# A four-layer attention and MLP kernel: three row tiles of layer 3 turned by DMA, its last residual rows in spent weights, and tile 5's key sums of layer 1 moved between tile 7's transposes and tile 6's second key half

## The chip, the cores and the metric

The kernel runs on one core of one Trainium2 chip. The metric is the time of one execution in microseconds of device time (us), as the median of several runs. Beside the runs there is one profiled execution, whose trace the views below are taken from.

## What is computed

The input x has 2048 rows of 576 numbers in bf16. Four layers are applied in the order A, B, A, B, each with its own layer norm in front and a residual sum behind. Both A layers share one set of weights, and so do both B layers.

```python
def A(x, wqkv, wo):                       # x: [2048, 576], 32 heads of 18
    q, k, v = split(x @ wqkv)
    phi = lambda t: where(t > 0, t + 1, exp(t)) + 1e-6
    pq, pk = phi(q), phi(k)
    kv = einsum("hsd,hse->hde", pk, v);  z = pk.sum(rows)
    return (pq @ kv) / (pq . z + 1e-6) @ wo      # by head
def B(x, w1, b1, w2, b2):                 # F = 4608
    return gelu(layernorm(x) @ w1 + b1) @ w2 + b2
x = x + A(layernorm(x)); x = x + B(x); x = x + A(layernorm(x)); x = x + B(x)
```

## The kernel before

The text calls the four layers layer 1 (A), 2 (B), 3 (A) and 4 (B); in the code they are li = 0, 1, 2, 3. The rows are cut into 16 row tiles of 128 rows (t = 0 to 15), and into four chunks of 512 rows (c = 0 to 3) of four tiles each.

**Normalised and turned rows.** Every layer's products read the normalised rows turned, so that features lie on partitions; they stand in `yT`. A pipe of small steps, `LNPipe`, takes each tile through statistics (VectorE's bn_stats at L456 and L457, or ScalarE's two passes at L430 and L443), the power on GpSimd (L492), the normalisation (GpSimd at L506 or L527, or VectorE at L510 or L531), and the turning. A tile is turned by five TensorE transposes and a copy out of PSUM ("act": L569, then ScalarE at L575), by a transposing DMA ("xbar": L553 or L558), or by VectorE and two DMAs through DRAM ("dma": L352, L362, L377). Each call of `lnp.tick` moves every waiting tile one step; `hold` is a number of ticks that a tile waits first, `tp_at` is the output tile (state["wo"]) before which it is not turned, `gap` holds a tile between ScalarE's two passes, and `stats` says which engine makes the statistics. Three row buffers, `y_ring`, hold normalised rows that are to be turned.

**An attention layer.** For each tile `k_half` makes the two halves of the keys (L753, k_ps) with the columns from KO on of `wqkv_sb`; `rows_by_keys` adds the products of rows and keys into accumulators (L800; the trace writes k_ps and k_tail); `q_proj` makes the queries (L719 and L724, q_ps), group by group. ScalarE's exponentials and identity passes (L619, L641, L645) and VectorE (L621, L651, L653) turn products into feature maps. PSUM tiles with the tag "h" are a ring of four banks, and a product waits until the bank's last reader is done. After the keys come the value products `kv_groups` (L853, kv_ps, with the columns from VO on of `wqkv_sb`), the denominators (L935), their spreading over the heads (L963, L977, copied by ScalarE at L981 and L965), the scaling of the query features by VectorE (L987 and L966), and the products with wo (L883).

**The output stage.** `wo_stage(t)` makes ten products for tile t (L1125, wo_ps) in one of two accumulators, accA for even and accB for odd tiles, and `residual` adds the tile's residual rows on VectorE (L695) and stores the sum to DRAM, to `x_d` (L702). In layer 3 the residual rows come from `x_d` by `prefetch_xo` (L671) into the nine buffers of the pool `rows`; at first eight of these hold the normalised rows of layer 3, and each is released by the key sums of its pair of tiles. Six loads stand ahead of the stage; the load of tile t + 5 stands ahead of output tile t for t = 1 to 10. From tile 9 on the loads take over the buffers of tiles 0, 1, 2 and so on, when their rows have been stored and normalised, and each stands behind the store before it. The first four tiles of the output stage go into the pipe at once, because the MLP's first chunk needs them. In layer 1 tiles 0 to 2 are turned by DMA and tile 3 by TensorE; in layer 3 all four are turned by TensorE:

```python
if li == 0:
    hold, tp_at, by_act = ((2, 0, 4, 6)[t], (5, 7, 8, 12)[t], t > 0)
else:
    hold, tp_at, by_act = ((2, 5, 8, 8)[t], (6, 9, 12, 13)[t], t in (1, 2))
```

**An MLP layer.** `m1_group` makes four blocks of the hidden layer (L1242; h_ps in the ring of banks, hp_ps in accA or accB, starting with accA), ScalarE applies gelu (L1238), and after nine groups the second product runs (L1306, m_ps). The rows of the next chunk are loaded from `x_d` (L423), normalised and turned meanwhile.

**Order.** TensorE's instructions run in the order in which the program calls them. The other engines' order is made by a scheduler, with hints that put one instruction behind another. All DMAs are issued by SyncE, one after the other: a DMA that waits for a buffer holds all that stand behind it.

Of the kernel before, what the change touches and what calls it, by code (L numbers as in the profile page):

```python
# [8 lines left out]
ALU = mybir.AluOpType  # L9
BF16 = mybir.dt.bfloat16  # L10
F32 = mybir.dt.float32
# [5 lines left out]
NT = S // P  # L17
# [10 lines left out]
KO, VO = QW, QW + D + 8  # L28
# [6 lines left out]
HALF = D // 2  # L35
# [6 lines left out]
def build(tc, A_x, A_wqkv, A_wo, B_w1, B_b1, B_w2, B_b2, out, dbg=None, n_layers=4):  # L42
    nc = tc.nc
    dbg = dbg or {}
    with ExitStack() as ctx:
# [102 lines left out]
        wqkv_sb = const.tile([P, KD, QW + 2 * D + 8], BF16, name="wqkv_sb")  # L148
# [12 lines left out]
        AHEAD = 4  # L161
        XB = 8
        BY_ACT = (13,)
        turned = const.tile([P, D // 32, TPC, 32], BF16, name="turned")
        x_d = dpool.tile([NT, P, D], F32, name="x_d")
# [13 lines left out]
        NOSYNC = mybir.DependencyInfo(mybir.DependencyClass.NoSync, mybir.DependencyReason.SCHED_ONLY)  # L179
# [216 lines left out]
        class LNPipe:  # L396
            def __init__(self):
                self.items = []

            def feed(self, xt, t, kind, norm_eng, evac_eng="dve", load_from=None, after=None, hold=0, stats="dve", tp_at=0, gap=0):  # L400
                self.items.append(dict(stage=(0 if load_from is None else -1), xt=xt, t=t, kind=kind,
                                       norm=norm_eng, evac=evac_eng, load=load_from,
                                       after=after, hold=hold, stats=stats, tp_at=tp_at, gap=gap))

            def busy(self):
                return len(self.items)
# [1 line left out]
            def tick(self, transposes=1):  # L408
                land()
                for it in list(self.items):  # L410
# [10 lines left out]
                    if st == -1:  # L421
                        xn = row_tile("xl")
                        load = nc.sync.dma_start(out=xn[:], in_=x_d[it["load"]])  # L423
                        if it["after"] is not None:
                            tc.add_manual_dep(load.ins, it["after"], NOSYNC, reason="loads give way")
                        it["xt"] = xn
                    elif st == 0 and it["stats"] == "act":
                        mv = it["mv"] = work.tile([P, 2], F32, name="ln_mv", bufs=6)
                        it["dump"] = blk.tile([P, D], BF16, name="ln_dump", tag="blk")
                        one = nc.scalar.activation(out=it["dump"][:], in_=it["xt"][:, 0:D], func=ACT.Identity,  # L430
                                                   scale=-1.0 / D, accum_out=mv[:, 0:1])
                        if it["after"] == "rden":
                            tc.add_manual_dep(one.ins, act_last["copy"], NOSYNC, reason="scalings first")
                        elif it["kind"] == "A":
                            tc.add_manual_dep(one.ins, act_last["exp"], NOSYNC, reason="keys go on first")
                        it["stage"] = 0.5
                        if it["kind"] == "B" and it["evac"] != "xbar":
                            it["hold"] = it["gap"]
                            continue
                    if it["stage"] == 0.5:  # L440
                        u = it["u"] = work.tile([P, 1], F32, name="ln_u", bufs=4)
                        mv = it["mv"]
                        two = nc.scalar.activation(out=it.pop("dump")[:], in_=it["xt"][:, 0:D], func=ACT.Square,  # L443
                                             bias=mv[:, 0:1], accum_out=mv[:, 1:2])
                        if it["gap"]:
                            tc.add_manual_dep(two.ins, act_last["copy"], NOSYNC, reason="scalings first")
                        act_last["stats"] = two.ins.name
                        scale, add = (1.0 / D, EPS) if it["kind"] == "A" else ((1.0 + EPS) / D, EPS * EPS)
                        nc.gpsimd.tensor_scalar(out=u[:], in0=mv[:, 1:2], scalar1=scale, scalar2=add,
# [141 lines left out]
        lnp = LNPipe()  # L591
# [68 lines left out]
            larger()  # L660

        xo_of = {}

        def prefetch_xo(li, t, add_b2):
            if li == 0:
                xo = blk.tile([P, D], BF16, name="xo_first", tag="blk")
                chained(nc.sync.dma_start(out=xo[:], in_=x_in[t * P:(t + 1) * P, :]))
                xo_of[(li, t)] = xo[:]
                return
            xo = row_tile("xo")  # L670
            load = nc.sync.dma_start(out=xo[:], in_=x_d[t])  # L671
            if not add_b2:
                behind(load, "landed")
                if t >= 9:
                    tc.add_manual_dep(load.ins, sp_last["store"], NOSYNC, reason="stores first")
            if add_b2:
                tc.add_manual_dep(load.ins, dve_last["sum"], NOSYNC, reason="no residual rows ahead of their stage")
                nc.gpsimd.tensor_tensor(out=xo[:], in0=xo[:], in1=b2_bc[:], op=ALU.add)  # L678
            xo_of[(li, t)] = xo[:]

        def residual(li, t, halves):
            xo = xo_of.pop((li, t))
            last = (li == n_layers - 1)
            if last:
                xn = rows.tile([P, 2 * D], BF16, name="xbf", tag="row")[:, 0:D]
            elif li == 0:
                xn = row_tile("xn")[:]
            else:
                xn = xo
            parts = LAST_PARTS if last and t == NT - 1 else [slice(0, D)]  # L690
            for i, cols in enumerate(parts):
                if len(parts) == 2:
                    total = nc.vector.tensor_tensor(out=xn[:, cols], in0=halves[i][:, 0:cols.stop - cols.start], in1=xo[:, cols], op=ALU.add)
                else:
                    total = nc.vector.tensor_tensor(out=xn[:, cols].rearrange("p (h n) -> p h n", h=2), in0=halves,  # L695
                                                    in1=xo[:, cols].rearrange("p (h n) -> p h n", h=2), op=ALU.add)
                dve_last["sum"] = total.ins.name
                if last:
                    nc.sync.dma_start(out=out_f[t * P:(t + 1) * P, cols], in_=xn[:, cols])
            if last:  # L700
                return None
            sp_last["store"] = nc.sync.dma_start(out=x_d[t], in_=xn).ins.name  # L702
            return xn

        def layer_A(li, next_kind, pre_a1=None):
# [286 lines left out]
            if li == 0:  # L992
# [36 lines left out]
                for t in range(4, NT):  # L1029
                    if t in (4, 5):  # L1030
                        k_half(t, 0)
                        (first_max if t == 4 else largest)(dve_after=dve_last["phi"])
                        k_half(t, 1)
                        if t == 4:
                            in_order("u5 s6a s6b g6 u6 ma40 ma41")
                    elif t == XB - 2:
                        k_half(t, 0)
                        pre_a1(t)
                        k_half(t, 1)
                    else:  # L1040
                        keys(t)
                    if t != XB - 2:
                        pre_a1(t)
                    if t == 4:
                        lnp.tick(transposes=0)
                    masks(2)
                    if t > 4:
                        rows_by_keys(t - 1, 0)
                    else:
                        for one in range(4):  # L1050
                            rows_by_keys(one, 0, (4,))
                    behind_keys = act_last["turned"] if t <= XB or act_last["stats"] is None else act_last["stats"]
                    if t != 6:
                        largest = q_proj(*q_left.pop(0), defer=True)(after=behind_keys, late=t == 4)
                    lnp.tick(transposes=0)
# [3 lines left out]
            else:  # L1059
                for t in range(6, NT - TPC):  # L1060
                    load_row(t)
                for t in range(NT):
# [9 lines left out]
                    if t:  # L1072
                        rows_by_keys(t - 1, 0)
                rows_by_keys(NT - 1, 0)

            last_rows_by_keys()
            left = list(range(NT))
# [51 lines left out]
            def wo_stage(t):  # L1129
                wo_products(t, WO_ORDER[wo_open[t][0] if t in wo_open else 0:])  # L1130
                wp = wo_open[t][1]
                xn = residual(li, t, wp[:, :, 0:HALF])
                if xn is not None and next_kind == "B" and t < TPC:
                    if li == 0:
                        hold, tp_at, by_act = ((2, 0, 4, 6)[t], (5, 7, 8, 12)[t], t > 0)
                    else:
                        hold, tp_at, by_act = ((2, 5, 8, 8)[t], (6, 9, 12, 13)[t], t in (1, 2))
                    lnp.feed(xn, t, "B", "pool", "xbar" if li == 0 and t < 3 else "act", hold=hold, tp_at=tp_at, gap=int(li > 0 and t == 2),
                             **(dict(stats="act", after="rden") if by_act else dict(after="sum")))

            for t in range(AHEAD + 2):
                prefetch_xo(li, t, add_b2=False)
# [3 lines left out]
            kv_groups((1, 2, 3))  # L1146
            quarter_scale(1, (2,), after=dve_last["mask"])
            phi = q_proj(*q_left.pop(0), defer=True)
            for g in (1, 2, 3):
                kv_wo_half(g, 0, by_dve=1 - g % 2)  # L1150
            wo_products(0, WO_ORDER[0:2])
# [3 lines left out]
            last_phi = phi  # L1155
            for t in range(NT):
                c, j = divmod(t, TPC)
                if li == 0 and t + AHEAD + 2 < NT or 0 < t < NT - AHEAD - 1 and li > 0:
                    prefetch_xo(li, t + AHEAD + (1 if li > 0 else 2), add_b2=False)
                wo_stage(t)  # L1160
                total = dve_last["sum"]
# [191 lines left out]
        for li, kind in enumerate(kinds):  # L1353
            nk = kinds[li + 1] if li + 1 < n_layers else None
            if kind == "A":
                if li == 0:
                    layer_A(li, nk, pre_a1=pre_a1_layer0)
                else:
                    def pre_a1(t):
                        lnp.tick()  # L1360
# [56 lines left out]
```

## Time and profile before

| | |
|---|---|
| three runs | 751.07, 751.93, 751.80 us; median 751.8 us |
| profiled execution | 751.45 us, of which the span from the first to the last instruction is 749.7 us |
| TensorE busy | 744.3 us, 6536 matmuls |
| VectorE, ScalarE, GpSimd busy | 260.0, 314.8, 119.2 us |
| granted TensorE clock | 1.000 |
| DMA | 75.72 MB, mean 101 GB/s |

In a timeline row stand the start and the length in us, the engine (PE is TensorE's matmuls, PEld its weight loads, DVE VectorE, ACT ScalarE, POOL GpSimd, SPq SyncE's queue of DMA issues), the line, the operation, what is written and read, the shapes, the number of instructions, and in brackets the idle time before them with what ended it. Rows of equal instructions are merged. The chain of waits gives start, length, engine, tile and line of the work that set the end. Names lose their numbers, so that k_ps stands for several tiles. In the table by stretches the columns are the stretch, the sum, the busy time of TensorE, its weight loads, VectorE, ScalarE and GpSimd, each with its instructions, the granted clock, the busy share of DMA and GB/s.

### The profile page before, as it was taken

The page shows a single profiled execution, that of the slowest core. Times are in us where ns is not written, and L with a number is a line of the kernel's source. Part 1 is how long each engine was busy: PE and PEld are TensorE (multiplying, and loading weights), DVE is VectorE, ACT ScalarE, POOL GpSimd, SP SyncE. Part 2 cuts the span into 40 slices and gives each one's busy share as a digit, 9 for nine tenths or more (in the row PEclk, how much of TensorE's full clock was granted, in tenths as well). Part 3 has the DMA queues.
Part 4 walks back from the last instruction along what each step waited for, and adds up shares of the span by engine and source line. Part 5 has one row for each costly group of instructions (what it writes and reads, how often), then busy time and mean ns, then how long its engine had stood idle before and what let it go on. Part 6 is the DMA issues. An engine that isn't in the chain of part 4 may idle for free.

```text
span 749.7 us, 15678 instructions
## 1 busy us (share of the span) xinstructions
PE 744.3 (99%) x6536; PEld 477.5 (64%) x6536; DVE 260.0 (35%) x641; ACT 314.8 (42%) x703; POOL 119.2 (16%) x224
## 2 busy tenths in 40 slices
PE   8999999999999999999999999999999999999998
PEld 5666744774576467546776767567646754774476
DVE  7867824235034404301367576600330041000000
ACT  5766756007501740373057665650263046105600
POOL 4831502003011201301100023300120020002000
PEclk9999999999999999999999999999999999999999
DMA  8797993227213701411404148420330033011000
GB/s 207 193 230 178 261 342 72 65 70 196 64 41 105 183 26 48 127 49 32 128 23 119 50 142 298 128 70 17 124 86 2 27 115 84 9 32 56 2 13 20
DMA packets 88529, 75.72 MB, mean 101 GB/s; under 512 B 44986, under 2 KB 73098, under 8 KB 88458
## 3 DMA queue, kind: packets, MB, share of 16 engines
q1 hardware_dynamic: 88458, 74.72, 35.7%
q8 instruction: 51, 0.84, 0.5%
q14 instruction: 20, 0.16, 0.1%
HBM read 48.10 MB, written 24.77 MB: 97 GB/s over the span
## 4 chain that ended last, share of the span: by engine, by line
PE 98%; DMA 1%; SPq 0%; issue 0%; ACT 0%; DVE 0%
PE m_ps L1306 37%; PE h_ps L1242 20%; PE hp_ps L1242 17%; PE wo_ps L1125 5%; PE k_ps L753 5%; PE q_ps L719 5%; PE k_ps L800 4%; PE m_half L1306 1%; DMA wqkv_sb<-in_A_wqkv_dram 1%; PE q_ps L724 1%; PE k_tail L800 1%; PE tp L569 0%; PE kv_ps L853 0%; PE kvwo_half L883 0%; PE den_ps L935 0%; PE rden_ps L977 0%
## 5 line engine op out<-in xcount | busy, mean ns | idle before, releaser
L1306 PE MATMUL m_ps<-w_sb,hT 128*128 128x288 bf16 x2232 | 274.8, 286 | 0.0
L1306 PEld LDWEIGHTS <-hT 128*128 128x128 bf16 x2304 | 224.3, 98 | 60.4 <-issue 3.4
L1242 PEld LDWEIGHTS <-w_sb 64*128 64x128 bf16 x2304 | 126.1, 94 | 134.1 <-issue 2.3
L1242 PE MATMUL hp_ps<-yT,w_sb 64*128 64x512 bf16 x1152 | 174.5, 376 | 0.0
L1242 PE MATMUL h_ps<-yT,w_sb 64*128 64x512 bf16 x1152 | 151.2, 376 | 0.0
L1247 ACT COPY relay_sb<-relay_sb 128x1 f32<-128x1 f32 x144 | 28.5, 198 | 261.3 <-PE h_ps L1242 218.7
L1238 ACT ACTIVATE hT<-h_ps,b1T 128x512 bf16<-128x512 f32 x144 | 91.2, 684 | 44.4 <-PE h_ps L1242 44.4
L1238 ACT ACTIVATE hT<-hp_ps,b1T 128x512 bf16<-128x512 f32 x144 | 91.2, 693 | 0.0
L492 POOL TENSOR_TENSOR ln_rstd<-ln_u,neg_half 128x1 f32<-128x1 f32 x62 | 34.3, 555 | 349.8 <-DVE ln_u L474 214.9
L695 DVE TENSOR_TENSOR xbf<-m_ps,xo 128x576 bf16<-128x576 f32 x15 | 11.4, 758 | 211.8 <-PE m_ps L1306 211.8
L695 DVE TENSOR_TENSOR xo<-m_ps,xo 128x576 f32<-128x576 f32 x16 | 12.1, 758 | 167.3 <-PE m_ps L1306 167.3
L678 POOL TENSOR_TENSOR xo<-xo,b_bc 128x576 f32<-128x576 f32 x32 | 41.0, 1283 | 106.9 <-DMA xo<-x_d 97.4
L1242 PE MATMUL h_ps<-yT,w_tail 64*128 64x512 bf16 x144 | 54.1, 376 | 0.0
L1242 PE MATMUL hp_ps<-yT,w_tail 64*128 64x512 bf16 x144 | 54.1, 376 | 0.0
L753 PE MATMUL k_ps<-wqkv_sb,yT 128*128 128x288 bf16 (+1 forms) x320 | 44.7, 286 | 1.2 <-DMA wqkv_sb<-in_A_wqkv_dram 0.9
L1125 PE MATMUL wo_ps<-kvwo,pq 128*128 128x288 bf16 x320 | 42.4, 286 | 0.0
L719 PE MATMUL q_ps<-yT,wqkv_sb 128*128 128x512 bf16 x160 | 39.3, 379 | 0.0
L753 PEld LDWEIGHTS <-yT 128*128 128x128 bf16 x320 | 30.9, 98 | 11.9 <-DMA wqkv_sb<-in_A_wqkv_dram 1.0
L1242 PEld LDWEIGHTS <-w_tail 64*128 64x128 bf16 x288 | 27.1, 94 | 16.9
L1125 PEld LDWEIGHTS <-pq 128*128 128x128 bf16 x320 | 30.5, 98 | 8.5 <-DVE pq L987 0.3
L641 ACT ACTIVATE phi_e<-q_ps 128x512 bf16<-128x512 f32 (+1 forms) x38 | 21.6, 575 | 23.7 <-PE q_ps L719 20.9
L352 DVE STREAM_TRANSPOSE turned<-y_ring 128x576 bf16<-128x576 bf16 x40 | 30.3, 766 | 0.4
(162 smaller groups left out, 543.3 us busy)
## 6 DMA issues: line engine op xcount, KB each, us to landing
xo<-x_d SPq DMA_DIRECT2D x48, 288.0 KB
x_d<-xo SPq DMA_DIRECT2D x32, 288.0 KB
xl<-x_d SPq DMA_DIRECT2D x24, 288.0 KB
y_d<-turned SPq DMA_DIRECT2D x40, 144.0 KB
w_sb<-in_B_w_dram SPq DMA_DIRECT2D x6, 864.0 KB
yT<-y_d SPq DMA_DIRECT2D x10, 512.0 KB
w_sb<-in_B_w_dram SPq DMA_DIRECT2D x9, 512.0 KB
x_d<-xn SPq DMA_DIRECT2D x16, 288.0 KB
```

What stands on the lines that cost most here:

```text
L352: turn = nc.vector.transpose(out=turned[:, :, j, :], in_=y[:, 0:D])
L492: power = nc.gpsimd.tensor_tensor(out=rstd[:], in0=it["u"][:], in1=neg_half[:], op=ALU.pow)
L678: nc.gpsimd.tensor_tensor(out=xo[:], in0=xo[:], in1=b2_bc[:], op=ALU.add)
L695: total = nc.vector.tensor_tensor(out=xn[:, cols].rearrange("p (h n) -> p h n", h=2), in0=halves, in1=xo[:, cols].rearrange("p (h n) -> p ...
L719: pe(nc.tensor.matmul(qp[:], lhsT=wqkv_sb[:, k, g * P:(g + 1) * P], rhs=yT[:, k, c * CA:(c + 1) * CA], start=(k == 0), stop=(k == KD - 1)))
L753: pe(nc.tensor.matmul(kp[:, 0:n], lhsT=yT[:, k, t * P:(t + 1) * P], rhs=wqkv_sb[:, k, KH[half]:KH[half] + n], start=(i == 0), stop=(i == K ...
L800: pe(nc.tensor.matmul(dst, lhsT=lhsT, rhs=pk, start=(t == 0), stop=(t == NT - 1)))
L1125: pe(nc.tensor.matmul(wp[:, half, 0:HALF], lhsT=features, rhs=kvwo[slot][:, half * HALF:(half + 1) * HALF], start=(g == WO_ORDER[0]), stop ...
L1238: act_last["gelu"] = nc.scalar.activation(out=to, in_=ps, func=ACT.Gelu_apprx_tanh, bias=b1T[:, f:f + 1], scale=1.0).ins.name
L1242: mm = pe(nc.tensor.matmul(dst[n], lhsT=wt, rhs=mv, start=(seen[n] == 0), stop=(seen[n] == 8)))
L1247: relay = nc.scalar.copy(out=relay_sb[:, 1:2], in_=relay_sb[:, 0:1])
L1306: pe(nc.tensor.matmul(acc[half][:, 0:cols.stop - cols.start], lhsT=hT[f][:, j * P:(j + 1) * P], rhs=w2_sb[:, f, cols], start=(f == 0), sto ...
```

## The change

In layer 3 the first four tiles of the output stage get layer 1's settings: tiles 0 to 2 are turned by a transposing DMA, issued behind the stores of output tiles 5, 7 and 8, tile 3 by TensorE, and the statistics of tiles 1, 2 and 3 are made by ScalarE. The parameter `gap` goes.

The residual rows of tiles 12 to 15 in layer 3 no longer go through the pool `rows`. Those of 14 and 15 are loaded behind the last key sums into the key columns of `wqkv_sb`, those of 12 and 13 behind the last query product into its query columns; each takes 576 bf16 columns of two of the five weight blocks as 2 x 288 numbers of float32. VectorE's sum writes in place, and the store to `x_d` reads from there.

In layer 1 the key sums of tile 5 stand between tile 7's transposes and the second key half of tile 6, instead of behind that key half.

```diff
@@ LNPipe
-            def feed(self, xt, t, kind, norm_eng, ..., tp_at=0, gap=0):
+            def feed(self, xt, t, kind, norm_eng, ..., tp_at=0):
...
-                            it["hold"] = it["gap"]
...
-                        if it["gap"]:
-                            tc.add_manual_dep(two.ins, act_last["copy"], NOSYNC, reason="scalings first")
@@ residual rows
+        SPENT = {15: (0, KO), 14: (2, KO), 13: (0, 0), 12: (2, 0)}
...
+            if not add_b2 and t in SPENT:
+                k, start = SPENT[t]
+                xo = wqkv_sb[:, k:k + 2, start:start + 2 * HALF].bitcast(F32)
+                nc.sync.dma_start(out=xo, in_=x_d[t].rearrange("p (h n) -> p h n", h=2))
+                xo_of[(li, t)] = xo
+                return
@@ residual
-                    total = nc.vector.tensor_tensor(out=xn[:, cols].rearrange("p (h n) -> p h n", h=2), in0=halves,
-                                                    in1=xo[:, cols].rearrange("p (h n) -> p h n", h=2), op=ALU.add)
+                    by_halves = [ap if len(ap.shape) == 3 else ap.rearrange("p (h n) -> p h n", h=2) for ap in (xn, xo)]
+                    total = nc.vector.tensor_tensor(out=by_halves[0], in0=halves, in1=by_halves[1], op=ALU.add)
...
-            sp_last["store"] = nc.sync.dma_start(out=x_d[t], in_=xn).ins.name
+            home = x_d[t] if len(xn.shape) == 2 else x_d[t].rearrange("p (h n) -> p h n", h=2)
+            sp_last["store"] = nc.sync.dma_start(out=home, in_=xn).ins.name
@@ layer_A, li == 0
                         k_half(t, 0)
                         pre_a1(t)
+                        rows_by_keys(t - 1, 0)
                         k_half(t, 1)
...
-                    if t > 4:
+                    if t == XB - 2:
+                        pass
+                    elif t > 4:
                         rows_by_keys(t - 1, 0)
@@ layer_A, li > 0, behind the last rows_by_keys(NT - 1, 0)
+                for t in (14, 15):
+                    prefetch_xo(li, t, add_b2=False)
@@ wo_stage
-                    if li == 0:
-                        hold, tp_at, by_act = ((2, 0, 4, 6)[t], (5, 7, 8, 12)[t], t > 0)
-                    else:
-                        hold, tp_at, by_act = ((2, 5, 8, 8)[t], (6, 9, 12, 13)[t], t in (1, 2))
-                    lnp.feed(xn, t, "B", "pool", "xbar" if li == 0 and t < 3 else "act", hold=hold, tp_at=tp_at, gap=int(li > 0 and t == 2),
-                             **(dict(stats="act", after="rden") if by_act else dict(after="sum")))
+                    lnp.feed(xn, t, "B", "pool", "xbar" if t < 3 else "act", hold=(2, 0, 4, 6)[t], tp_at=(5, 7, 8, 12)[t],
+                             **(dict(stats="act", after="rden") if t > 0 else dict(after="sum")))
@@ behind the last q_proj
+            if li > 0:
+                for t in (12, 13):
+                    prefetch_xo(li, t, add_b2=False)
...
-                if li == 0 and t + AHEAD + 2 < NT or 0 < t < NT - AHEAD - 1 and li > 0:
+                if li == 0 and t + AHEAD + 2 < NT or 0 < t < min(SPENT) - AHEAD - 1 and li > 0:
```

More of the change, by code (lines that the diff above doesn't have):

```diff
@@ L398, in __init__, with feed @@
                 self.items = []
-            def feed(self, xt, t, kind, norm_eng, evac_eng="dve", load_from=None, after=None, hold=0, stats="dve", tp_at=0, gap=0):
+            def feed(self, xt, t, kind, norm_eng, evac_eng="dve", load_from=None, after=None, hold=0, stats="dve", tp_at=0):
                 self.items.append(dict(stage=(0 if load_from is None else -1), xt=xt, t=t, kind=kind,
                                        norm=norm_eng, evac=evac_eng, load=load_from,
-                                       after=after, hold=hold, stats=stats, tp_at=tp_at, gap=gap))
+                                       after=after, hold=hold, stats=stats, tp_at=tp_at))
             def busy(self):
```

## The prediction

> **What bounds the kernel now.** I read the page first, then what TensorE waited for, then the chain of work in the three stretches that the edits touch, then the queues that feed those stretches. The page:
>
> ```profile
> span 749.7 us, 15678 instructions
> PE 744.3 (99%) x6536; PEld 477.5 (64%) x6536; DVE 260.0 (35%) x641; ACT 314.8 (42%) x703; POOL 119.2 (16%) x224
> ```
>
> TensorE is busy for 744.3 of 749.7 us, so an edit pays only by taking TensorE instructions away or by closing a hole in its stream. The view of waits, for TensorE, names one hole near an edit:
>
> ```profile
> PE k_ps L753 <- ACT phi_a L645: 0.3, 1, 0.3
> ```
>
> Busy time hides small holes, since a matmul row lasts longer than the distance to the next one. So I measure from start to start. The chain in time order through layer 3's output stage into layer 4 (start, length, what):
>
> ```profile
> 442.21 1.96 PE wo_ps L1125 x16
> ...
> 451.80 0.28 PE tp L569 x5
> 452.08 1.23 PE wo_ps L1125 x10
> ...
> 461.83 0.28 PE tp L569 x5
> 462.10 2.45 PE wo_ps L1125 x20
> 464.56 1.18 PE h_ps L1242 x9
> 465.74 1.14 PE hp_ps L1242 x9
> 466.88 0.88 PE h_ps L1242 x9
> ```
>
> TensorE runs through: each of four groups of five transposes (first and last shown) costs 0.28 us in line, between output products. Layer 1's output stage has the arrangement that the change gives to layer 3: three tiles turned by DMA, one on TensorE. The same view there:
>
> ```profile
> 74.74 1.96 PE wo_ps L1125 x16
> ...
> 92.28 0.28 PE tp L569 x5
> ...
> 96.24 1.18 PE h_ps L1242 x9
> 97.42 0.87 PE hp_ps L1242 x9
> ```
>
> From the same product group to the first MLP matmul it takes 96.24 - 74.74 = 21.50 us; layer 3 takes 464.56 - 442.21 = 22.35 us.
>
> **Layer 3: the transposes.** Three groups of five leave TensorE: 3 x 0.28 = 0.84 us, all on the path. The copies of the turned tiles leave ScalarE, and tile 3's statistics move from VectorE to ScalarE. Both engines are off the path, and in the built program their order through this stage becomes layer 1's but for two swapped statistics instructions. 22.35 - 0.84 = 21.51 agrees with layer 1's 21.50, which ran with that order: I take 0.84. If the cover of layer 1's example did not hold, a late scaling would show as a hole before output products.
>
> **Layer 3: the residual rows.** After the first MLP products comes the first pair tile (hp_ps). Layer 2 passes from it to the next h_ps in 0.87 us (97.42 row), layer 4 in 1.14 us (465.74 row): 0.27 us more. The pair tile takes the accumulator of output tile 14. VectorE's timeline for the sums of tiles 14 and 15:
>
> ```profile
> 464.83 0.76 DVE L695 TENSOR_TENSOR xo<-wo_ps,xo 128x576 f32<-128x576 f32 x1 [1.95 <-DMA xo<-x_d]
> 466.26 0.76 DVE L695 TENSOR_TENSOR xo<-wo_ps,xo 128x576 f32<-128x576 f32 x1 [0.67 <-DMA xo<-x_d]
> ```
>
> The sum of tile 14 stood 1.95 us waiting for its residual rows, ended at 465.59, and the pair tile could begin only then. The change loads rows 14 and 15 into the keys' weights and rows 12 and 13 into the queries' weights, stages earlier, so this wait goes: 0.27 us. Without it the removal of the transposes would have been given back here. Next late is layer 2's pattern, which shows no hole. The bounds are 0 (another hole takes its place) and 0.27; I take 0.27.
>
> These loads pass others on SyncE's queue. 14 and 15 stand behind load 0 and ahead of load 1, and in the built program the value product (kv_ps) now waits for them, though it reads other columns. The nearest rows: SyncE, TensorE, and one microsecond of the table by stretches (last number GB/s):
>
> ```profile
> 425.63 9.89 SPq L671 DMA_DIRECT2D xo<-x_d  x7
> ...
> 430.23 0.73 PE L853 MATMUL kv_ps<-k,wqkv_sb 128*72 128x72 bf16 x10
> ...
> 427.00:428.00 1.00, 1.00 (x44) 0.74 (x43) 0.00 (x0) 0.02 (x1) 0.00 (x0) 1.00 0.79 249
> ```
>
> Load 1 leaves at 425.63 and 249 GB/s pass between 427 and 428, most of a tile (128 x 576 x 4 bytes = 0.295 MB). Even if the two new loads left only then, they would be in by about 429.5, ahead of 430.23. They wait for the last key product and should leave earlier. Cost 0; if the cover fails, below. Loads 12 and 13 wait for the last query product and precede the first store, which needs a later sum: 0. Stores 12 to 15 write from two half rows each, and nobody on the path waits for them: 0.
>
> **Layer 3: the DMA transposes.** They are new on SyncE's queue, behind stores 5, 7 and 8, and the first MLP weight load waits for all three. SyncE in layer 1, where they stand behind the same stores:
>
> ```profile
> 84.66 2.00 SPq L553 DMA_TRANSPOSE yT<-y_ring  x1
> ...
> 88.33 1.24 SPq L553 DMA_TRANSPOSE yT<-y_ring  x1
> ...
> 90.77 1.25 SPq L553 DMA_TRANSPOSE yT<-y_ring  x1
> ```
>
> The DMA view for 93 to 93.5 us and for 94 to 94.5 us shows when the last one's small packets end:
>
> ```profile
> DMA packets 250, 0.06 MB, mean 122 GB/s; under 512 B 250, under 2 KB 250, under 8 KB 250
> ...
> DMA packets 123, 0.16 MB, mean 330 GB/s; under 512 B 12, under 2 KB 91, under 8 KB 123
> ```
>
> They are through by about 94.0, so 3.2 us after issue, and 2.2 us before 96.24. Layer 3's stage maps onto layer 1's with an offset of 464.56 - 0.84 - 96.24 = 367.48 us: the last transpose leaves at 458.25, its packets end at 461.5, and the matmuls need them at 463.7. I take 0. In layer 3 they stand behind the loads of tiles 10 and 11, which wait for the norms of tiles 1 and 2 to release row buffers. That is the risk. Upper bound of a landing, from the rows of tiles 14 and 15:
>
> ```profile
> 459.72 0.38 SPq L671 DMA_DIRECT2D xo<-x_d  x1
> ...
> 460.73 0.46 SPq L671 DMA_DIRECT2D xo<-x_d  x1
> ```
>
> 460.73 to the sum at 466.26 is 5.5 us; with that the last transpose lands at 458.25 + 5.5 = 463.75, still without a hole worth counting.
>
> The Trainium skill, VectorE: DVE Perf Modes, sections "The three transpose paths" and "Rules for kernel authors", speaks against this edit: it gives 390 ns for a 128x128 transpose on TensorE and 1309 ns by DMA, and says to use TensorE where PSUM will do. By it, as an estimate, 15 x 390 ns = 5.9 us would leave TensorE, and five blocks by DMA would land 6.5 us after issue, 1.1 us too late. The rows disagree on both: 0.28 us for five, and 3.2 us for a whole tile under traffic.
>
> **Layer 1: tile 6's second key half.** It goes behind tile 5's key sums; tile 7's transposes, already ahead of it, stay. The timeline:
>
> ```profile
> 24.83 0.44 PE L569 MATMUL tp<-ident,x 128*128 128x128 bf16 x5
> 24.91 0.59 ACT L645 ACTIVATE phi_a<-q_ps 128x512 bf16<-128x512 f32 x1
> 25.55 0.77 PE L753 MATMUL k_ps<-wqkv_sb,yT 128*128 128x288 bf16 x5 [0.28 <-ACT phi_a L645]
> 25.68 0.71 ACT L575 COPY yT<-tp 128x640 bf16<-128x640 bf16 x1
> 26.16 0.45 DVE L621 SCALAR_TENSOR_TENSOR pk<-k_ps,phi_e 128x289 bf16<-128x289 f32 x1
> 26.16 0.29 PE L800 MATMUL k_tail<-pk,x 128*65 128x289 bf16 x1
> 26.78 1.39 PE L753 MATMUL k_ps<-wqkv_sb,yT 128*128 128x289 bf16 x10
> ```
>
> Five transposes take 0.28 us, so TensorE was free at 25.11; the key half waited for a bank until 25.55: 0.44 us lost. The key sums (five matmuls, 26.16 to 26.78 = 0.62 us) need nothing from it and fill 25.11 to 25.73; the key half follows to 26.34 (25.55 to 26.16 = 0.61). Then tile 7's keys, first at 26.78, have two waits: their turned rows (25.68 + 0.71 = 26.39) and the bank that VectorE frees at 26.16 + 0.45 = 26.61. I start them at 26.66 and gain 0.12 us. Bounds: 0, if VectorE is later by that much, and 0.44, if the bank is free earlier.
>
> **Sum.** 0.84 + 0.27 + 0.12 = 1.23 us. The profiled execution took 751.45 us (749.7 of span and 1.75 around it): 750.22. It lies 0.35 under the median of the three runs, 751.8, from which the same sum gives 750.57. I say 750.4, between the two; the span would be 748.5.
>
> **Rivals.** First, slower: the queue holds the transposes. The normalisations of tiles 1 and 2 on GpSimd, before (layer 3) and in layer 1:
>
> ```profile
> 453.25 0.82 POOL L527 TENSOR_SCALAR y_ring<-xo,ln_rstd,ln_nmr 128x576 bf16<-128x576 f32 x1
> ...
> 458.26 0.82 POOL L527 TENSOR_SCALAR y_ring<-xo,ln_rstd,ln_nmr 128x576 bf16<-128x576 f32 x1
> ...
> 83.69 0.82 POOL L527 TENSOR_SCALAR y_ring<-xn,ln_rstd,ln_nmr 128x576 bf16<-128x576 f32 x1
> ...
> 86.31 0.82 POOL L527 TENSOR_SCALAR y_ring<-xn,ln_rstd,ln_nmr 128x576 bf16<-128x576 f32 x1
> ```
>
> With layer 1's timing tile 2's ends at 86.31 + 0.82 + 367.48 = 454.6; if it stayed where it is, load 11 would leave at 459.1, and two transposes (1.25 us each) and three stores behind it would put the last issue near 462, its landing at 465.2 (3.2 us) to 467.5 (5.5 us). That is a hole of 1.5 to 3.8 us against a gain of 1.23: 751.7 to 754.0, about 753. It is slower by over 0.2% (1.5 us, about what a measurement of this kernel can tell from no change) once the hole exceeds 2.7 us. Against it: tile 2's statistics now stand ahead of the second set of scaling copies on ScalarE. I give 0.09.
>
> Second, the value product waits for rows 14 and 15. Leaving at 425.63 and landing 5.5 us after the second issue (about 426.2), they hold it from 430.23 to 431.7: 1.5 us, so 751.45 - 1.23 + 1.5 = 751.7. Against it: DMA is idle then. I give 0.06, and 0.03 for a worse hole of the same kind.
>
> Third, only the transposes count: layer 1 gains nothing and another wait replaces tile 14's: 751.45 - 0.84 = 750.6. I give 0.12.
>
> Fourth, more: layer 1 gains the whole 0.44 us, because tile 7's keys find their bank free when TensorE comes to them. 0.84 + 0.27 + 0.44 = 1.55 us; 751.45 - 1.55 = 749.9. The row at 26.16 speaks against it: VectorE reaches that bank only then. I give 0.12.
>
> The forecast keeps 0.58. That the edits do nothing has no chance worth naming: the transposes are on the chain.
>
> **Numbers.** Faster by over 0.2% is below 750.3 from the median's 751.8. The forecast, 750.57 by that count, lies 0.27 above, and the three runs of before spread over 0.86 us (751.07 to 751.93), so I count a third of it (0.19) and two thirds of the fourth rival (0.08) as faster, with 0.02 of the third: 0.29. Slower: most of the first rival and the worse part of the second, and a remainder: 0.11. Same: 0.60. Range: below, 751.07 - 1.55 = 749.5; above, the value product's wait and part of the first rival, 752.0.
>
> **What would show it.** In the chain: one group of transposes in layer 3's output stage, 21.5 us from its product group to the first h_ps, and 0.87 us for the first hp_ps. VectorE's sums of tiles 14 and 15 follow TensorE, not DMA. In layer 1 the wait for phi_a is gone and tile 7's keys start near 26.66. It is wrong if TensorE waits at the first MLP matmul or at kv_ps for a DMA, or if products of output tiles 12 to 13 wait for a sum.

## The result and the profile after

The changed kernel takes 750.30 us (median of 22 runs, 749.68 to 750.82); before, in the same comparison, 751.52 us (22 runs, 750.73 to 752.62). The ratio is 0.9984, with a 95% interval of 0.9977 to 0.9990: 1.22 us, 0.16%. The forecast was 750.4 us, by a sum of 1.23 us.

The page after the change, and from the view of what TensorE waited for the line that is new:

```profile
span 748.4 us, 15645 instructions
PE 741.9 (99%) x6507; PEld 473.5 (63%) x6521; DVE 259.1 (35%) x637; ACT 314.2 (42%) x704; POOL 121.1 (16%) x225
...
PE k_ps L758 <- DVE pk L618: 0.2, 1, 0.2
```

The span is 1.3 us shorter. Weight loads fall by 15, the three groups of five transposes; 14 further matmul records are missing from this trace. The wait for phi_a in layer 1 is gone; a shorter one for VectorE stands in its place. The chain through layer 3's output stage (start, length, what):

```profile
441.77 1.96 PE wo_ps L1135 x16
...
453.01 6.23 PE wo_ps L1135 x50
459.24 0.28 PE tp L566 x5
459.52 3.67 PE wo_ps L1135 x30
463.19 1.18 PE h_ps L1251 x9
464.38 0.87 PE hp_ps L1251 x9
465.24 1.07 PE h_ps L1251 x9
```

One group of transposes is left. From the 16 products to the first h_ps it takes 463.19 - 441.77 = 21.42 us, 0.93 less than before, and the first pair tile takes 0.87 us, 0.27 less. VectorE's sums of tiles 14 and 15 now follow TensorE, not DMA:

```profile
462.01 0.76 DVE L700 TENSOR_TENSOR wqkv_sb<-wo_ps,wqkv_sb 128x576 f32<-128x576 f32 x1 [0.47 <-PE wo_ps L1135]
463.23 0.76 DVE L700 TENSOR_TENSOR wqkv_sb<-wo_ps,wqkv_sb 128x576 f32<-128x576 f32 x1 [0.47 <-PE wo_ps L1135]
```

SyncE's queue and the value product, in the timeline:

```profile
420.53 1.24 SPq L671 DMA_DIRECT2D wqkv_sb<-x_d  x2
...
429.78 0.72 PE L858 MATMUL kv_ps<-k,wqkv_sb 128*72 128x72 bf16 x10
...
452.42 1.37 SPq L550 DMA_TRANSPOSE yT<-y_ring  x1
...
455.46 1.68 SPq L550 DMA_TRANSPOSE yT<-y_ring  x1
...
457.98 1.23 SPq L550 DMA_TRANSPOSE yT<-y_ring  x1
```

Rows 14 and 15 leave 9 us ahead of the value product, which does not wait. The last transpose leaves at 457.98, 5.21 us ahead of the first h_ps, which does not wait either.

Layer 1, first VectorE before, then TensorE and VectorE after:

```profile
25.54 0.70 DVE L653 TENSOR_TENSOR pq<-phi_a,phi_e 128x512 bf16<-128x512 bf16 x1 [0.18 <-ACT phi_a L645]
```

```profile
24.35 0.44 PE L566 MATMUL tp<-ident,x 128*128 128x128 bf16 x5
...
25.05 0.77 DVE L650 TENSOR_TENSOR pq<-phi_a,phi_e 128x512 bf16<-128x512 bf16 x1 [0.20 <-ACT phi_a L642]
...
25.75 0.45 DVE L618 SCALAR_TENSOR_TENSOR pk<-k_ps,phi_e 128x289 bf16<-128x289 f32 x1
...
26.25 1.39 PE L758 MATMUL k_ps<-wqkv_sb,yT 128*128 128x289 bf16 x10 [0.23 <-DVE pk L618]
```

From tile 7's transposes to its keys it was 26.78 - 24.83 = 1.95 us and is 1.90 us. TensorE comes to the keys earlier, and waits until VectorE has freed the bank (25.75 + 0.45 = 26.20).

### The profile page after: what moved, and what is told of

It reads as the page before. It is cut to its first block, busy times and chain, and to the rows that moved or that the text cites. A ratio compares the mean times of both kernels' runs of the same rounds, so it can differ in the third digit from the quotient of the medians.

```text
span 748.4 us, 15645 instructions
## 1 busy us (share of the span) xinstructions
PE 741.9 (99%) x6507; PEld 473.5 (63%) x6521; DVE 259.1 (35%) x637; ACT 314.2 (42%) x704; POOL 121.1 (16%) x225
## 4 chain that ended last, share of the span: by engine, by line
PE 98%; DMA 1%; SPq 0%; issue 0%; DVE 0%; ACT 0%
PE m_ps L1315 37%; PE h_ps L1251 21%; PE hp_ps L1251 17%; PE wo_ps L1135 5%; PE k_ps L758 5%; PE q_ps L724 5%; PE k_ps L805 4%; PE m_half L1315 1%; PE q_ps L729 1%; DMA wqkv_sb<-in_A_wqkv_dram 1%; PE k_tail L805 1%; PE kv_ps L858 0%; PE kvwo_half L888 0%; PE den_ps L940 0%; PE rden_ps L982 0%; PE k_tail L845 0%
## 5 line engine op out<-in xcount | busy, mean ns | idle before, releaser
L1251 PEld LDWEIGHTS <-w_sb 64*128 64x128 bf16 x2304 | 124.5, 94 | 136.5 <-issue 1.9
L1251 PE MATMUL hp_ps<-yT,w_sb 64*128 64x512 bf16 x1152 | 178.0, 376 | 0.0
L1251 PE MATMUL h_ps<-yT,w_sb 64*128 64x512 bf16 x1152 | 147.9, 376 | 0.0
```

Source lines behind the costliest of these rows:

```text
L1251: mm = pe(nc.tensor.matmul(dst[n], lhsT=wt, rhs=mv, start=(seen[n] == 0), stop=(seen[n] == 8)))
```

## Experiments

The table gives TensorE's starts by the chain: the 16 products of layer 3's output stage, the first h_ps and the first m_ps of layer 4 (for the kernel marked *, h_ps is from the timeline). Stage is h_ps less products, both parts m_ps less products. A chain row behind a wait starts with its first matmul, any other 0.06 to 0.07 us behind it (after: 463.19, in the timeline 463.13). So the stages of the kernel marked * and of the last three rows, whose h_ps waits, are that much short against the others; both parts has no such step.

| kernel | 16 products | h_ps | stage | m_ps | both parts |
|---|---|---|---|---|---|
| before | 442.21 | 464.56 | 22.35 | 499.90 | 57.69 |
| before_again_1 | 441.82 | 464.17 | 22.35 | 499.24 | 57.42 |
| before_again_2 | 442.39 | 464.74 | 22.35 | 500.01 | 57.62 |
| e_keys_only | 441.56 | 465.10 | 23.54 | 500.18 | 58.62 |
| e_spent_only | 442.12 | 464.47 | 22.35 | 499.54 | 57.42 |
| e_dma_turn_only * | 442.07 | 464.40 | 22.33 | 500.26 | 58.19 |
| after | 441.77 | 463.19 | 21.42 | 498.26 | 56.49 |
| after_again | 441.48 | 462.90 | 21.42 | 497.97 | 56.49 |
| e_layer3_only | 441.70 | 463.13 | 21.43 | 498.20 | 56.50 |
| e_pk_first | 441.69 | 463.12 | 21.43 | 498.19 | 56.50 |
| e_pk_bias | 441.46 | 462.89 | 21.43 | 497.96 | 56.50 |
| e_turn2_at9 | 441.77 | 463.52 | 21.75 | 498.66 | 56.89 |
| e_turn2_at11 | 441.52 | 464.33 | 22.81 | 499.48 | 57.96 |
| e_four_dma | 441.75 | 464.00 | 22.25 | 499.14 | 57.39 |

**Layer 1's edit alone** (e_keys_only).

```diff
 # before, li == 0, t == XB - 2
                         k_half(t, 0)
                         pre_a1(t)
+                        rows_by_keys(t - 1, 0)
                         k_half(t, 1)
```

> The kernel before with the layer-1 edit alone (tile 5's key sums between tile 7's transposes and tile 6's second key half). Theory: TensorE no longer waits for phi_a (0.3 us), but waits for the bank that VectorE frees instead; from tile 7's transposes to tile 7's keys it was 1.95 us (24.83 to 26.78) and becomes 1.83 to 1.90 us; the gain is 0.05 to 0.12 us, which the time cannot show. Rival (the whole wait is won): 1.51 us, a gain of 0.44 us. Layer 3's stage stays at 22.35 us and layer 4's first hp_ps at 1.14 us in both.

751.22 us against 751.25, ratio 1.0001 (0.9991 to 1.0010). Tile 7's keys come 26.12 - 24.22 = 1.90 us behind its transposes. From those transposes to the next k_tail it takes 3.17 or 3.18 us in all five traces with the old order, 3.07 to 3.13 us in all seven with the new one alone: a gain of 0.05 us, once 0.1, at the low end of what was expected. The rival is out. Layer 3's stage, whose code is that of before, did not stay at 22.35 us:

```profile
462.91 0.76 DVE L695 TENSOR_TENSOR xo<-wo_ps,xo 128x576 f32<-128x576 f32 x1 [2.43 <-DMA xo<-x_d]
...
463.72 1.39 PE L1128 MATMUL wo_ps<-kvwo,pq 128*128 128x288 bf16 x10 [1.03 <-DVE xo L695]
```

A sum waited 2.43 us for its residual rows (DVE L695), and the last output product 1.03 us for that sum.

**The kernel before, twice more** (before_again_1, before_again_2), to see whether that belongs to the edit.

> The kernel before once more, for the spread of its layer 3. From the 16 output products to m_ps its profile took 57.69 us, and the kernel with the layer-1 edit alone, with the same layer 3, 58.62. Theory: the late residual rows of tiles 13 to 15 make this stretch vary from one execution to the next, between 57.6 and 58.7 us. Rival: layer 1's edit lengthened it, and before gives 57.69 again.

> The kernel before a third time, for the same spread: 57.6 to 58.7 us by the theory, 57.69 by the rival.

750.83 and 751.58 us. Both parts took 57.42 and 57.62 us. The spread is there, lower than expected: the late rows cost 0, 0.20 and 0.27 us in three executions of before and 1.20 us in e_keys_only, counted from 57.42, the time without them. None of the three shows the large hole. The traces say where it came from. Counted from the 16 products, SyncE issues the store ahead of tile 13's load at 12.73 us in all four executions. That store lands (the last of its sixteen semaphore updates in the trace) at 16.61, 16.47 and 16.57 us in before and at 17.33 us in e_keys_only, and the load leaves 0.01 to 0.02 us behind it each time. SyncE's issues in this stage up to that store, and the work of GpSimd and ScalarE, stand at the same times within 0.01 us. So the large hole comes from a store that took 0.7 to 0.9 us longer to land, not from an instruction that came later. That speaks against the edit; why the store took longer is not shown.

**Layer 3's edits alone** (e_layer3_only): the changed kernel without the line that e_keys_only adds.

> The changed kernel with layer 1's order as before: both edits of layer 3 and nothing else. Theory: the whole gain but 0.05 us is here. Layer 3's stage 21.4 us (22.35 before), first hp_ps of layer 4 0.87 us (1.14 before), sum 1.2 us, so a ratio near 0.9984. Rival (the difference of the two profiles, among it 0.48 us at the start, belongs to layer 1's edit): the first key products start at 8.46 us again, and the time is within 0.6 us of before.

750.26 us against 751.25, ratio 0.9988 (0.9979 to 0.9996). Both parts take 56.50 us: all of layer 3's gain is here. The first group of ten key products, which stands ahead of every edit, starts at 7.88 us here, with layer 1's old order; it started at 8.46 before and at 7.98 in the changed kernel. So those 0.48 us are no effect of the edits. In all 14 traces tile 7's transposes start between 24.19 and 24.86 us.

**DMA transposes without the spent weights** (e_dma_turn_only).

```diff
 # after
-        SPENT = {15: (0, KO), 14: (2, KO), 13: (0, 0), 12: (2, 0)}
+        SPENT = {}
 # and the loads of tiles 12 to 15 back in the loop over t
```

> The changed kernel, but all residual rows of layer 3 go through the row buffers as before; the three DMA transposes stay. Theory (the transposes' gain is given back at tile 14's residual rows): stage 21.4 us as in the changed kernel, but the sum of tile 14 is still bound by the DMA, so the first hp_ps of layer 4 grows from 1.14 us to at least 1.9 us, and the net gain is 0.1 us or less, or a loss if the loads of tiles 14 and 15, now behind the transposes on SyncE's queue, leave later than 459.72 and 460.73. Rival (the transposes count by themselves): hp_ps stays at 1.14 us and 0.9 us are won, ratio 0.9988.

751.70 us against 751.25, ratio 1.0006 (0.9997 to 1.0014). TensorE and VectorE in the timeline:

```profile
462.14 0.76 DVE L700 TENSOR_TENSOR xo<-wo_ps,xo 128x576 f32<-128x576 f32 x1 [1.75 <-DMA xo<-x_d]
...
462.95 1.39 PE L1133 MATMUL wo_ps<-kvwo,pq 128*128 128x288 bf16 x10 [0.68 <-DVE xo L700]
...
465.19 0.76 DVE L700 TENSOR_TENSOR xo<-wo_ps,xo 128x576 f32<-128x576 f32 x1 [2.29 <-DMA xo<-x_d]
...
466.00 1.04 PE L1246 MATMUL hp_ps<-yT,w_sb 64*128 64x512 bf16 x8 [0.36 <-DVE xo L700]
```

Two holes behind residual rows, one more than expected. The expected one is smaller than expected: the first pair tile starts 466.00 - 464.40 = 1.60 us after the first h_ps, 1.15 us in before, so 0.45 us later, not 0.76 us (1.9 less 1.14) or more. A third, of 0.13 us, stands ahead of the first h_ps: by its semaphore updates the last transpose landed only at 464.27, 5.05 us after its issue. On SyncE's queue (next fence) the two loads now stand behind transposes:

```profile
459.22 1.34 SPq L550 DMA_TRANSPOSE yT<-y_ring  x1
460.67 0.71 SPq L675 DMA_DIRECT2D xo<-x_d  x1
...
461.91 1.21 SPq L675 DMA_DIRECT2D xo<-x_d  x1
```

They left at 459.72 and 460.73 before, and leave at 460.67 and 461.91. Both parts take 58.19 us, 1.70 over after: more than the transposes' gain is given back. The medians of the same comparison say so too: 751.70 us against 750.26 for e_layer3_only, which differs from this kernel by the spent weights and by layer 1's 0.05 us. The rival (0.9 us won) is out.

**Spent weights without the DMA transposes** (e_spent_only): before with `SPENT`, its four loads and the sum in place; the four groups of TensorE transposes stay.

> The kernel before with the residual rows of tiles 12 to 15 of layer 3 in spent weights; the four TensorE transposes of layer 3 and layer 1's order stay. Theory: stage of layer 3 between 22.25 and 22.35 us, first hp_ps of layer 4 0.87 us instead of 1.14, so 0.27 us won, 0.1 us more if the small hole at tile 12's products belongs to late residual rows. Rival: another wait takes the place of tile 14's (hp_ps stays above 1.0 us), or kv_ps waits for the new loads (its start later than 430.23 by more than 0.1 us).

751.12 us against 751.25, ratio 0.9997 (0.9988 to 1.0006). hp_ps passes in 0.87 us, and the stage stays at 22.35 us: the extra 0.1 us did not come. So the spent weights by themselves win only what the late rows cost in that execution, and the transposes, once no row is late, 57.42 - 56.49 = 0.93 us. Neither rival showed.

**The last transpose later** (e_turn2_at9, e_turn2_at11): in layer 3 `tp_at` of tile 2 is 9 or 11 instead of 8.

> The changed kernel with layer 3's last DMA transpose one output tile later. In the changed kernel it leaves at 457.98 and its small packets end at about 461.0, 2.1 us ahead of the first MLP matmul (463.19). Theory (a transpose lands 3.1 us after issue, and nobody waits before 463.2): it leaves near 459.4, lands near 462.5, no hole: stage 21.4 us, time as the changed kernel. Rival (the queue or the traffic of the last stores slows it to 5.5 us): it lands at 464.9, a hole of 1.7 us before the first MLP matmul.

> The changed kernel with layer 3's last DMA transpose three output tiles later. Theory (3.1 us from issue to landing): it leaves near 462.4, lands near 465.5, and the first MLP matmul, which waits for all three, starts 2.3 us late; layer 3's stage 23.7 us and the time 2.3 us over the changed kernel, that is 1.1 us over before: the price that the first rival named. Rival (landing 5.5 us after issue): a hole of 4.7 us. Other rival (the MLP's weight load does not bind the first matmul): no hole.

At 9 it is 750.09 against 750.99 us, ratio 0.9984 (0.9975 to 0.9994), the changed kernel's ratio; at 11 it is 751.18 us, ratio 0.9999 (0.9990 to 1.0008). At 9, by SyncE's queue, the chain and TensorE:

```profile
458.34 1.63 SPq L550 DMA_TRANSPOSE yT<-y_ring  x1
...
458.34 5.14 DMA yT<-y_ring
...
463.52 1.04 PE L1251 MATMUL h_ps<-yT,w_sb 64*128 64x512 bf16 x8 [0.32 <-DMA yT<-y_ring]
```

The transpose left only 0.36 us later than in the changed kernel, and in this execution TensorE waited for it: it was released 5.14 us after the issue, and both parts are 0.40 us longer. At 11:

```profile
459.88 1.90 SPq L550 DMA_TRANSPOSE yT<-y_ring  x1
...
464.33 1.04 PE L1251 MATMUL h_ps<-yT,w_sb 64*128 64x512 bf16 x8 [1.39 <-DMA x_d<-xo]
```

It left 1.90 us later, not 4.4, and the matmul came 4.45 us after the issue; both parts are 1.47 us longer. The profile names a store as releaser, but only the transpose was moved, and the trace has the sixteen semaphore updates with which each transpose ends: the last came 4.36 us after the issue, 0.09 us ahead of the matmul. The landing lies between theory (3.1 us) and rival (5.5 us).

The same updates tell how much slack the changed kernel has. In the five traces with its settings for this transpose (after, after_again, e_layer3_only, e_pk_first, e_pk_bias) it lands 3.43, 3.97, 4.60, 4.80 and 3.34 us after its issue, which is 1.72, 1.31, 0.47, 0.33 and 2.06 us ahead of the first h_ps in the timeline. So the slack changes from one execution to the next, and 0.36 us of delay would have opened a hole of some 0.1 us in one of these five and none in the others; in e_turn2_at9 the landing itself was late.

Where the time went shows in the DMA view, of after first (460.5 to 461, 461 to 461.25), then of e_turn2_at9 (461.25 to 461.5, 461.5 to 461.75, 462.25 to 462.5):

```profile
DMA packets 209, 0.16 MB, mean 324 GB/s; under 512 B 159, under 2 KB 159, under 8 KB 208
...
DMA packets 42, 0.10 MB, mean 387 GB/s; under 512 B 0, under 2 KB 0, under 8 KB 42
```

```profile
DMA packets 65, 0.06 MB, mean 241 GB/s; under 512 B 43, under 2 KB 43, under 8 KB 65
...
DMA packets 4, 0.01 MB, mean 37 GB/s; under 512 B 0, under 2 KB 0, under 8 KB 4
...
DMA packets 8, 0.00 MB, mean 8 GB/s; under 512 B 8, under 2 KB 8, under 8 KB 8
```

A tile is 640 packets of 256 bytes (128 x 640 x 2 bytes). In after they end by 461.0, 3.0 us after issue (3.2 by the prediction), and the transpose lands at 461.41, 0.5 us behind the last one. In e_turn2_at9 all but sixteen are through by 461.5, 3.1 us after issue; the queue then stands nearly still, the last sixteen come between 462.17 and 462.65, and the release follows at 463.48, 0.8 us behind them. What held them back is not shown. The Trainium skill, DMA: Bandwidth & Descriptors, section "Anatomy of one DMA", says, for DMAs that GpSimd issues, that most of some 2 us of fixed cost lies behind the last byte, in the confirmation ahead of the semaphore; here, on SyncE's queue, 0.5 and 0.8 us lie behind it.

**Tile 3 by DMA too** (e_four_dma).

```diff
 # after, wo_stage
-  "xbar" if t < 3 else "act", ..., tp_at=(5, 7, 8, 12)[t]
+  "xbar" if t < 3 or li > 0 else "act", ..., tp_at=(5, 7, 8, 12 if li == 0 else 9)[t]
```

> The changed kernel with layer 3's tile 3 turned by DMA as well, right behind tile 2. Its normalisation ends near 457.4, so it leaves after tile 2's issue at about 459.3 and lands near 462.4 to 463. Theory: the last group of five transposes leaves TensorE, 0.28 us; stage 21.14 us; the landing is just in time for 462.9. Rival (two transposes in a row slow each other and the stores): they land late, a hole before the first MLP matmul of more than 0.28 us, time equal or slower than the changed kernel.

750.44 us against 750.99, ratio 0.9990 (0.9981 to 0.9999).

```profile
460.04 2.08 SPq L550 DMA_TRANSPOSE yT<-y_ring  x1
...
464.00 1.04 PE L1251 MATMUL h_ps<-yT,w_sb 64*128 64x512 bf16 x8 [1.10 <-issue]
```

0.28 us less on TensorE, 1.10 us of hole: both parts are 0.90 us longer than in the changed kernel. The rival's outcome holds: it lands late. It left at 460.04, 0.7 us later than expected, and its last semaphore update comes 3.87 us after the issue, 0.09 us ahead of the matmul; tile 2's transpose, in the same trace, took 4.70 us. That two in a row slow each other is not shown: the last transpose of the five traces above took up to 4.80 us without a second one behind it.

**VectorE's order in layer 1** (e_pk_first): `largest` for tile 5's query is called behind tile 6's first key half.

```diff
 # after, li == 0
                     elif t == XB - 2:
                         k_half(t, 0)
+                        largest(dve_after=dve_last["phi"])
...
-  largest = q_proj(*q_left.pop(0), defer=True)(after=behind_keys, late=t == 4)
+  largest = q_proj(*q_left.pop(0), defer=True)(after=behind_keys, late=t in (4, 5))
```

> The changed kernel, but VectorE takes the maximum of tile 6's first key half (pk) ahead of the query's maximum (pq) in layer 1. In the changed kernel pq (0.77 us) stands ahead of it and TensorE waits until 26.25 for the bank. Theory (that queue order is what kept the gain of layer 1 at 0.05 instead of 0.44): pk starts when its exponential is ready, about 25.35, ends about 25.80, and tile 7's keys start when their turned rows are copied, about 25.95: 1.6 us after tile 7's transposes instead of 1.90, 0.3 us won in the trace. Rival (another wait behind it: the copy of the turned rows or the next banks): 0.1 us or less, or a new wait a tile later.

750.06 us against 750.99, ratio 0.9983 (0.9974 to 0.9992).

```profile
25.20 2.12 PE L758 MATMUL k_ps<-wqkv_sb,yT 128*128 128x288 bf16 x15
...
25.31 0.46 DVE L618 SCALAR_TENSOR_TENSOR pk<-k_ps,phi_e 128x289 bf16<-128x289 f32 x1 [0.50 <-ACT phi_e L616]
...
25.68 0.42 DVE L650 TENSOR_TENSOR pq<-phi_a,phi_e 128x512 bf16<-128x512 bf16 x1
```

15 key products run without a wait. Tile 7's k_tail comes 27.15 - 24.30 = 2.85 us behind its transposes, 3.13 in after: 0.28 us more is won. In this trace it was lost again at the output stage of layer 1:

```profile
71.07 0.33 POOL L319 CAST b1T<-b_raw 128x36 f32<-128x36 bf16 x1 [27.01 <-DMA b_raw<-in_B_b_dram]
...
73.32 0.53 PE L1136 MATMUL wo_ps<-kvwo,pq 128*128 128x288 bf16 x3 [0.26 <-POOL kvwo L894]
```

GpSimd's cast of a bias waited for its DMA, and the copies for the products stood behind it. The same late copies stand in e_spent_only and before_again_2, so this edit is not needed for them.

**The cast behind the copies** (e_pk_bias, beside after_again).

```diff
 # e_pk_first; pool_last["kvwo"] is the second copy into kvwo
-  tc.add_manual_dep(cast.ins, pool_last["norm"], NOSYNC, ...)
+  tc.add_manual_dep(cast.ins, pool_last["kvwo"], NOSYNC, ...)
```

> The changed kernel with the maximum of tile 6's first key half ahead of the query's, and with GpSimd's cast of the MLP bias (b1T) behind its two kvwo copies. The trace with the first of these alone won 0.28 us at tile 7's keys and lost 0.3 us at layer 1's first output products, because the copies stood behind the cast and the cast behind the bias's DMA. Theory: both go; from tile 7's transposes to layer 1's first h_ps it takes 71.15 us instead of 71.4, and the time lies 0.3 us under the changed kernel of this call. Rival: another wait stands behind (the next GpSimd work, or a tile later), and the stretch stays at 71.4.

> The changed kernel once more, beside the one above. Theory: from layer 3's 16 output products to the m_ps group of layer 4 it takes 56.5 us again (56.49, 56.50, 56.50 in three traces), since no residual load binds there any more. Rival: it varies as before's does.

749.48 us (749.26 to 749.92) and 750.09 us (749.83 to 750.45), against 750.95: ratios 0.9979 (0.9970 to 0.9988) and 0.9985 (0.9977 to 0.9994). It is 0.61 us under the changed kernel. Tile 7's transposes start at 24.40 and 24.22, layer 1's first h_ps at 95.48 and 95.50: 71.08 us against 71.28, so 0.20 us of it is seen in the traces. Another 0.3 us of span lies behind the start of TensorE's last group (11.88 us to the end, against 12.21); e_turn2_at9 has 11.86 us there without this edit, so the 0.3 us is not shown to be the edit's. after_again repeats 56.49 us.

## Why the prediction was right

**Transposes, 0.84 us.** 0.92 or 0.93 measured, in five traces. The three groups are 0.84; e_spent_only, where no row is late, keeps the other 0.09, so it isn't the residual rows. Most of it is a late scaling in before, where the prediction says that TensorE runs through. It shows in the weight loads of the output products (e_spent_only has the same wait):

```profile
459.41 0.60 PEld L1125 LDWEIGHTS <-pq 128*128 128x128 bf16 x6 [0.30 <-DVE pq L987]
```

Two neighbouring products start 0.28 us apart there, where others start 0.12 us apart. That hole of 0.16 us is gone in after, and one of 0.10 us stands at 451.07. So the agreement with layer 1's 21.50 us was partly luck: layer 1's stage has two small holes of its own, 0.10 us at 84.04 and 0.07 us at 90.70.

**Residual rows, 0.27 us.** Right in the two profiles compared, but the term is one draw: 0, 0.20 and 0.27 us in three executions of before. What the step did see, that without the spent weights the removal of the transposes would have been given back, is the main result: e_dma_turn_only loses 1.70 us against the changed kernel. The loads cost nothing, as argued; the second rival is out.

**DMA transposes, 0 us.** Right: no wait in the five traces with these settings. The step took the end of the small packets for the landing (461.5) and 2.2 us of slack. In after the landing came at 461.41 and the slack was 1.7 us; over the five traces it is 0.3 to 2.1 us, so a slack of 2.2 us is about the best of the draws. The upper bound of 5.5 us in the same step covers all of them. Of the first rival only the second half showed: a late transpose makes a hole (e_turn2_at11: 1.47 us for an issue 1.90 us late). Its first half, a late normalisation of tile 2 that holds load 11, did not come: that ended at 454.22, predicted 454.6. The Trainium skill, VectorE: DVE Perf Modes, section "The three transpose paths", gives the figures from which the prediction estimated 5.9 us less on TensorE and 6.5 us to the landing; measured were 0.93 us, and 3.3 to 5.1 us.

**Layer 1, 0.12 us.** 0.05 measured. The mechanism and the next wait were the ones named; VectorE's maximum before it took 0.77 us instead of 0.70, which is the difference. The fourth rival's 0.44 us needs the bank free earlier: with VectorE's order changed 0.28 us more came.

**Sum.** -0.05 in layer 1, +0.08 in layer 1's output stage (21.58 against 21.50 us), -0.93 and -0.27 make -1.17 us. With the start (-0.48 us) TensorE's last group of products comes 1.64 us earlier (737.84 before, 736.20 after); what stands behind it took 0.34 us longer, so the span is 1.3 us shorter. Neither was traced to the change: from that group to the end of the span it takes 11.90 us in before, and with the edits 12.22 us in after, but 11.86 us in e_turn2_at9. That forecast and median agree within 0.01 us (1.23 and 1.22) is therefore partly luck: the residual rows were the largest of three draws, and terms outside the sum nearly cancel.

## What to carry to other kernels

Price a DMA from its issue to the release of its reader, and over several executions: in this kernel one transpose, at one place, landed 3.3 to 4.8 us after its issue. An edit that takes work off the path can be worth less than nothing alone, when loads stand next behind it; move them first, and measure each half by itself. A hole or a slack read from one trace is one draw: take two more executions before it becomes a term of a sum.

## What the chip showed that was not expected

A transposing DMA of one 128 x 640 tile landed 3.3 to 5.1 us after its issue in layer 3 (28 of them in nine traces), mostly 0.5 to 0.7 us behind its last 256-byte packet; in three of them one of the sixteen semaphore updates came 1.5 us or more after the other fifteen. Late residual rows cost 0 to 0.27 us in three executions of the same kernel, and its times spread over 1.9 us (22 runs), the changed kernel's over 1.1 us.
